# The last expert's rows reach the mixer's first batch through a product with a matrix of ones and zeros

## The chip, the cores and the metric

One core of one Trainium2 chip runs the whole program in one launch. The metric is the device time of the launch in microseconds (us). The engines are TensorE (PE; its weight loads are listed as PEld), VectorE (DVE), ScalarE (ACT), GpSimd (POOL) and SyncE (SP); each runs its own instructions in order and they meet at semaphores. SP issues nearly all plain transfers, POOL the indirect ones (gathers by a list of row numbers).

## The reference

An attention, a mixture of experts and a token and channel mixer follow each other on 4 batches of 576 tokens with 512 features:

```python
x = attention(q, k, v).transpose(0, 2, 1, 3).reshape(B, S, H * D)   # B=4, S=576, H*D=512
for b, s:                                        # experts: one expert e per token
    e = fresh_e if s == 0 or local_gate[b, s] < 0.5 else prev_e
    h = np.maximum(x[b, s] @ w1[e], 0.0)         # 512 -> 1024
    out[b, s] = p[e] * (h @ w2[e])               # 1024 -> 512, p = softmax of the gate
xt = out.transpose(0, 2, 1)                      # mixer
h = np.maximum(xt @ w_tok1, 0.0) @ w_tok2        # over tokens, 576 -> 256 -> 576
u = out + h.transpose(0, 2, 1)
return u + np.maximum(u @ w_ch1, 0.0) @ w_ch2    # over features, 512 -> 1536 -> 512
```

## The kernel before

Three stages use the chip one after another. Each stage records its operations in a `Sched`, which sets the order on every engine by a list of estimated costs and due times and by the buffers that each pool has; the order is fixed when the program is built. All of a helper's operations have the helper's line: L548 a product, L550 a transpose, L552 any other recorded operation, L1168 a gather, L1199 a load of expert weights.

**Experts** (`Moe`, some 200 to 425 us). The eight experts are taken by falling number of tokens; the place of an expert in that order is its rank, and `CAPS` gives the rows that each rank has room for (384, 376, 320, 288, 256, 256, 192 and 128). The routed rows lie in the DRAM table `xd` and are gathered into `xg`; for each rank the hidden size 1024 is cut into 8 chunks. A chunk is one 512 KB load `raw<-in_wx` (4 buffers, SP), its split into a rounded part `wh` (ACT) and a rest `wl` (DVE), a group of products into `m` (`mm1`), a relu with a split into `h` (ACT and DVE), and a group of products that adds into the PSUM banks `y` (`mm2`; four banks, one for each 128 rows of a rank). The last rank, with 128 rows, takes its first products from `raw` itself. After a rank's eighth chunk `mm2` copies each `y` into one of three buffers `yo` (ACT the even ones, DVE the odd ones) and SP stores them to the rank's rows in the DRAM table `yd` (`yd<-yo`, 256 KB each). Beside this, `convert` splits the mixer's weights: load `cr`, four DVE operations on `cf`, one of ACT on `cs`. `zeros()` fills the unused rows of `yd` from a buffer of its own, `zero`.

**Overflow** (L1545). Rows beyond a rank's room are worked off by a loop on the device, whose count `nov` is a runtime value. With these inputs it does not run once, but its start is a place where all engines meet and where SP first waits for every transfer that is still under way. `TAIL` (36) products on constants stand on PE ahead of it (L1537).

**Mixer** (`Mix`, 426 us to the end). For each batch, `token` brings the batch's 576 rows from `yd` in 5 tiles (128, 128, 128, 128 and 64 rows) by gathers with the index `pos`. Each tile is scaled by the gate's probability `pall` twice, on ACT into a rounded part (`f2x<-x_f,pall`) and on DVE in full; DVE subtracts to get the rest; PE transposes the tile (`x_t<-ident,x_f`) and multiplies it into the token mixing (`x_y`). A tile's six products of 128x512 need `f2x` and the rest `f3x`. Filler products on constants (L1752) stand between.

Of the kernel before, what the change touches and what calls it, by code (L numbers as in the profile page):

```python
# [4 lines left out]
F32 = mybir.dt.float32  # L5
F32R = mybir.dt.float32r
# [14 lines left out]
NB5 = 5  # L21
# [6 lines left out]
ROW0 = [128 * sum(TILES[:r]) for r in range(NE)]  # L28
NEARLY, ECAP = 2, 256
ETILES = ECAP // 128  # L30
EROW0 = [128 * sum(TILES) + ECAP * r for r in range(NEARLY)]
OV0 = 128 * sum(TILES) + ECAP * NEARLY
MIN_N = 256
NOV = 16
FF = 1024
# [1087 lines left out]


# [49 lines left out]
class Experts:  # L1174
# [87 lines left out]

    def part(self, C):
# [31 lines left out]
    def mm2(self, r, fb, h):  # L1295
# [27 lines left out]
        if fb == KF - 1:  # L1323
            for k in range(T):
                n = min(128, C - 128 * k)
                t = self.result(r, k)
                if n == m:
                    self.i("act", "copy", out=t[0:n], in_=self.y[k][n:2 * n])
                    self.i("dve", "tensor_tensor", out=t[0:n], in0=t[0:n], in1=self.y[k][0:n], op=ALU.add)
                elif k % 2 == 0:  # L1330
                    self.i("act", "copy", out=t[0:n], in_=self.y[k][0:n])
                else:
                    self.i("dve", "tensor_copy", out=t[0:n], in_=self.y[k][0:n])
                r0 = self.rows[r] + 128 * k
                self.i(self.QUEUE, "dma_start", out=self.yd[r0:r0 + n, :], in_=t[0:n])
# [115 lines left out]
class Moe(Experts):  # L1451
    LO, CUT, QUEUE = "dve", 4, "dma"

    def __init__(self, ctx, tc, at, rt, xd, yd, wx, jobs, lead):
        self.rt, self.xd, self.jobs = rt, xd, jobs
# [13 lines left out]
        for name, ts in tiles.items():  # L1469
            S_.pool(name, [ts[j] for j in sorted(ts)])  # L1470
        for name, n in (("t", 2), ("m", 2), ("y", 4)):
            S_.pool(name, [(pt if name == "t" else pp).tile([128, 512], F32, name=f"{name}{j}") for j in range(n)])
# [18 lines left out]

    def hidden(self, C):
        h, m = self.new("h"), self.part(C)
        return h[:, 0:C], h[:, C:2 * C], h[:, C - m:C + m] if m else None

    def zeros(self):

        zero = self.sp.tile([128, DM], F32, name="zero")
        self.S.i("pool", "memset", out=zero, value=0.0)
        for n in range(0, NOV, 2):  # L1500
            r0 = OV0 + 128 * n
            self.S.i("dma", "dma_start", out=self.yd[r0:r0 + 256, :].rearrange("(i p) w -> p i w", p=128),
                     in_=zero.unsqueeze(1).to_broadcast([128, 2, DM]))
        for r in range(NE):
            n = 128 * TILES[r] - CAPS[r]
            if n:
                self.S.i("dma", "dma_start", out=self.yd[ROW0[r] + CAPS[r]:ROW0[r] + CAPS[r] + n, :], in_=zero[0:n, :])

    def run(self):
# [3 lines left out]
        for n in range(NW):  # L1513
# [12 lines left out]
            if n == 24:  # L1526
                self.S.stage = t0
                self.zeros()
            if n >= 8 and n % CONV == 0 and self.jobs:
                self.S.stage = t0 + 60  # L1530
                convert(self.S, *self.jobs.pop(0), after=(done[n - 6],))
        self.mm2(*prev)
        assert not self.jobs
        self.S.issue(self.S.order(busy=LATE))
        at, cold = self.at, self.S.pools["t"][1][0][:, 264:512]
# [3 lines left out]
    def overflow(self):  # L1539
        tc, nc = self.tc, self.nc  # L1540
        rt, at, p = self.rt, self.at, {n: ts[0][0] for n, ts in self.S.pools.items()}
# [3 lines left out]
        with tc.For_i(0, nov, 1) as j:  # L1545
# [15 lines left out]
            for fb in range(KF):  # L1561
# [5 lines left out]
                h = self.S.pools["cs"][fb % 2][0][:, 0:128]  # L1567
# [4 lines left out]
            nc.sync.dma_start(out=self.yd[bass.ds(OV0 + j * 128, 128), :], in_=yo)  # L1572

# [11 lines left out]
class Mix:  # L1585


    def __init__(self, ctx, tc, at, rt, yd, out, c1, c2, c2t, wt):
# [10 lines left out]
        S_.slots(("f",), sp)  # L1599
        for name, n in (("t", 2), ("m", 2), ("y", 4)):  # L1600
            S_.pool(name, [pp.tile([128, 512], F32, name=f"x_{name}{j}") for j in range(n)])
# [42 lines left out]
    def token(self, b, after=()):  # L1644
# [6 lines left out]
        for j in range(NB5):  # L1651
            n = min(128, S - 128 * j)
            t = S_.next("f")
            gather(S_, t, n, self.yd[:, :], self.rt.pos[0:n, NB5 * b + j:NB5 * b + j + 1], after)
            p = self.at.pall[0:n, b, j:j + 1]
            s = t if b else S_.next("f")
            hi, lo = self.pair() if n == 128 else [S_.next("f", F32R)] * 2
            lo = lo if n == 128 else hi[n:2 * n]
            S_.tie(t, s, hi, lo)
            i("act", "activation", out=hi[0:n], in_=t[0:n], func=AF.Copy, scale=p)  # L1660
            i("dve", "tensor_scalar", out=s[0:n], in0=t[0:n], scalar1=p, scalar2=None, op0=ALU.mult)
# [94 lines left out]
def tile_kernel(tc, qT, kw, vw, vf, wcat, cst, wx, wt, c1, c2, out):  # L1756
    nc = tc.nc
    with ExitStack() as ctx:
# [4 lines left out]
        yd = dp.tile([OV0 + NOV * 128, DM], F32, name="yd")  # L1763
# [29 lines left out]
        for k in range(C2_EARLY):  # L1793
            jobs.append((c2[:, k], DM, *c2t[k]))
        with ExitStack() as a:
            moe = Moe(a, tc, at, rt, xd, yd, wx, jobs, lead)
            moe.run()
            moe.overflow()
        lead_stack.close()
        with ExitStack() as a:  # L1800
            Mix(a, tc, at, rt, yd, out, c1t, c2, c2t, wtt).run()
# [3 lines left out]
TAIL = 36  # L1805
# [8 lines left out]
RING_F, TOK_FB = 26, 3  # L1814
# [29 lines left out]
```

## Time and profile before

| | |
|---|---|
| time, median of 3 runs | 797.12 us (795.53 to 799.46) |
| the profiled execution: time / span | 797.57 us / 795.6 us |
| PE busy | 757.0 us, 95% |
| DVE / ACT / POOL busy | 468.0 (59%) / 333.1 (42%) / 95.4 (12%) us |
| DMA, mean over the span | 136 GB/s |

How to read the rows further down. A line of a timeline has its start and its duration in us, the engine, the line of the program, the operation with output<-inputs and shapes, a count where several stand in a row, and in brackets how long its engine was idle before it and what ended that. SPq is the issue of a transfer by SP. The records of products overlap: the distance of two starts is what a product costs. A line of windows has the stretch, its length, the busy time of PE, PEld, DVE, ACT and POOL (with the number of instructions), the granted clock of TensorE as a share of full speed, the share of the DMA engines and GB/s. In a line of the profile's costliest groups the last fields are busy time and mean ns of one, and the idle time before.

### The profile page before, as it was taken

The page shows a single profiled execution, that of the slowest core. Times are in us where ns is not written, and L with a number is a line of the kernel's source. Part 1 is how long each engine was busy: PE and PEld are TensorE (multiplying, and loading weights), DVE is VectorE, ACT ScalarE, POOL GpSimd, SP SyncE. Part 2 cuts the span into 40 slices and gives each one's busy share as a digit, 9 for nine tenths or more (in the row PEclk, how much of TensorE's full clock was granted, in tenths as well). Part 3 has the DMA queues.
Part 4 walks back from the last instruction along what each step waited for, and adds up shares of the span by engine and source line. Part 5 has one row for each costly group of instructions (what it writes and reads, how often), then busy time and mean ns, then how long its engine had stood idle before and what let it go on. Part 6 is the DMA issues. An engine that isn't in the chain of part 4 may idle for free. (4 is left out here: it accounts for less than half of the span.)

```text
span 795.6 us, 13989 instructions
## 1 busy us (share of the span) xinstructions
PE 757.0 (95%) x5377; PEld 639.8 (80%) x5377; DVE 468.0 (59%) x1093; ACT 333.1 (42%) x722; POOL 95.4 (12%) x100
## 2 busy tenths in 40 slices
PE   7888898799999999999998999999999999999997
PEld 5666686687798988888886888888788878888897
DVE  7779899598667779888953774532242224211121
ACT  1867876544455556565643442312221223011110
POOL 4335311314011010000002000010001000000000
PEclk9989999999999999999999999999999999999999
DMA  9998343649698676777762231020002000000010
GB/s 274 229 215 227 97 137 126 185 140 300 232 346 278 208 269 195 287 244 263 243 213 77 82 97 67 28 80 20 14 1 79 20 14 1 26 28 1 1 54 27
DMA packets 36346, 107.90 MB, mean 136 GB/s; under 512 B 5003, under 2 KB 5643, under 8 KB 35895
## 3 DMA queue, kind: packets, MB, share of 16 engines
q1 hardware_dynamic: 32359, 95.15, 37.4%
q0 software_dynamic: 3200, 10.28, 4.3%
q10 hardware_dynamic: 720, 1.57, 0.6%
q8 instruction: 43, 0.70, 0.4%
q14 instruction: 24, 0.20, 0.1%
HBM read 87.32 MB, written 19.66 MB: 134 GB/s over the span
## 5 line engine op out<-in xcount | busy, mean ns | idle before, releaser
L552 DVE SCALAR_TENSOR_TENSOR x_h<-x_m,x_h 128x512 fp32r<-128x512 f32 (+1 forms) x60 | 38.2, 638 | 194.4 <-ACT x_h L552 194.4
L548 PE MATMUL x_y<-x_h,c2h 128*128 128x512 f32 (+1 forms) x480 | 136.4, 369 | 0.0
L552 ACT ACTIVATE x_h<-x_m 128x512 fp32r<-128x512 f32 (+1 forms) x60 | 33.3, 555 | 206.6 <-PE x_m L548 181.6
L548 PEld LDWEIGHTS x_y<-x_h,c2h 128*128 128x128 f32 x480 | 86.5, 189 | 14.3
L548 PE MATMUL x_y<-x_h,c2l 128*128 128x512 f32 (+1 forms) x240 | 88.3, 368 | 0.0
L548 PE MATMUL y<-wh,h 128*128 128x512 f32 (+2 forms) x206 | 71.8, 400 | 0.2
L552 DVE TENSOR_TENSOR wl<-raw,wh 128x1024 fp32r<-128x1024 f32 (+1 forms) x48 | 54.8, 1143 | 21.6 <-ACT wh L552 20.9
L552 ACT CAST wh<-raw 128x1024 fp32r<-128x1024 f32 (+1 forms) x48 | 47.3, 986 | 31.7 <-PE y L548 25.3
L548 PEld LDWEIGHTS x_y<-x_h,c2l 128*128 128x128 f32 x240 | 45.3, 189 | 7.6
L548 PEld LDWEIGHTS y<-wh,h 128*128 128x128 f32 (+2 forms) x206 | 38.3, 186 | 9.2 <-DVE h L552 1.1
L548 PE MATMUL y<-wl,h 128*128 128x512 f32 (+3 forms) x112 | 41.5, 392 | 0.0
L552 ACT ACTIVATE h<-m 128x256 fp32r<-128x256 f32 (+6 forms) x64 | 25.6, 400 | 22.8 <-PE m L548 22.3
L1168 POOL DMA_INDIRECT xg<-xd,q_xi x19 | 19.4, 1019 | 127.3 <-PE t L550 111.9
L552 DVE SCALAR_TENSOR_TENSOR h<-m,h 128x256 fp32r<-128x256 f32 (+3 forms) x88 | 29.3, 357 | 4.1 <-ACT h L552 4.0
L548 PE MATMUL m<-l_xh,wh 128*128 128x256 f32 (+2 forms) x92 | 28.0, 305 | 1.7 <-DVE h L552 1.6
L548 PE MATMUL pv<-pt,vw 128*64 128x96 f32 x384 | 22.3, 261 | 7.6 <-ACT pt L552 4.6
L552 DVE SCALAR_TENSOR_TENSOR cf<-cr,cf 128x512 int32<-128x512 int32 (+1 forms) x42 | 28.4, 678 | 0.5
L548 PE MATMUL m<-l_xh,wl 128*128 128x256 f32 (+2 forms) x92 | 27.8, 302 | 0.6 <-DVE wl L552 0.6
L548 PEld LDWEIGHTS pv<-pt,vw 128*64 128x64 f32 x384 | 17.6, 142 | 12.6 <-ACT pt L552 5.5
L548 PE MATMUL m<-l_xl,wh 128*128 128x256 f32 (+2 forms) x92 | 27.6, 300 | 0.0
L548 PE MATMUL g<-wcat,xt 128*128 128x137 f32 x160 | 25.1, 299 | 2.0 <-ACT pd L552 1.1
L552 ACT COPY pt<-pc 32x384 f32<-32x384 f32 x48 | 24.4, 508 | 4.8 <-DVE pc L552 4.1
(803 smaller groups left out, 1954.6 us busy)
## 6 DMA issues: line engine op xcount, KB each, us to landing
raw<-in_wx SPq DMA_DIRECT2D x80, 512.0 KB
cr<-in_c SPq DMA_DIRECT2D x16, 512.0 KB
vw<-in_vw SPq DMA_DIRECT2D x12, 512.0 KB
kz<-in_kw SPq DMA_DIRECT2D x24, 200.0 KB
xd<-xn SPq DMA_DIRECT2D x16, 256.0 KB
yd<-zero SPq DMA_DIRECT2D x8, 512.0 KB
yd<-yo SPq DMA_DIRECT2D x15, 256.0 KB
x_cr<-in_c SPq DMA_DIRECT2D x7, 512.0 KB
```

Source lines behind the costliest of these rows:

```text
L548: f(kw.pop("out"), **kw)
L552: f(**kw)
L1168: nc.gpsimd.indirect_dma_start(out=t.real()[0:n, :], out_offset=None, in_=table, in_offset=bass.IndirectOffsetOnAxis(ap=index, axis=0))
```

## The change

- **Routing** makes three more tables for batch 0: `iota`, `place` (a token's place among the last rank's 128 rows, outside 0 to 127 for other tokens) and `pos0` (the token's row in `yd`, or the number of a row of zeros where the token belongs to the last rank).
- **The last rank's rows** move to the end of `yd`, so that a gather from `yd[0:ROW0[-1]]` does not depend on their store.
- **`select`** makes a 128x640 matrix `sel` of ones and zeros: five comparisons of `iota` with `place` on DVE, into two `yo` buffers, five transposes on PE and two copies on ACT.
- **`fetch0`** gathers batch 0's five tiles into `x_e0` to `x_e4` ahead of the loop's end, and ACT scales each by `pall`. They lie in a pool of their own, and serve the mixer as five more `f` buffers.
- **`add0`**, in place of nothing: the last rank's `y` is split into `yh` (ACT) and `yl` (DVE), ten products with `sel` spread its rows over the tokens of five tiles in PSUM, and five DVE operations add `pall` times those to `x_e`. The store of the last rank stays.
- **Mixer**: batch 0 has no gathers; `hi` is an ACT copy of `x_e`, and the DVE scaling is gone. Batches 1 to 3 are as before.
- **Space**: `cs` 2 to 1, `xg` 5 to 3, `RING_F` 26 to 21, no `zero` (`zeros()` uses a `yo`), `TAIL` 36 to 20. In the loop on overflow rows the five tiles are gathered again.

```diff
+        self.place = pp.tile([128, NB5], F32, name="place")
+        v("tensor_single_scalar", out=self.place, in_=row[:, 0:NB5], scalar=-float(ROW0[NE - 1]), op=ALU.add)
...
         if fb == KF - 1:
+            if self.last(r):
+                self.add0()
             for k in range(T):
...
-        zero = self.sp.tile([128, DM], F32, name="zero")
+        zero = self.S.next("yo")
...
+    def select(self):
+        S_ = self.S
+        for j0, j1 in ((0, 4), (4, NB5)):
+            ps = self.new("t").rearrange("p (k n) -> p k n", k=4)
+            a = self.new("yo").rearrange("p (k n) -> p k n", k=4)
+            for j in range(j0, j1):
+                S_.i("dve", "tensor_scalar", out=a[:, j - j0], in0=self.rt.iota, scalar1=self.rt.place[:, j:j + 1], scalar2=None, op0=ALU.is_equal)
+            with S_.group("pe"):
+                for j in range(j0, j1):
+                    S_.i("pe", "transpose", out=ps[:, j - j0], in_=a[:, j - j0], ident=self.ident)
+            S_.i("act", "copy", out=self.sel[:, 128 * j0:128 * j1], in_=ps[:, 0:j1 - j0].rearrange("p k n -> p (k n)"))
+
+    def fetch0(self):
+        S_ = self.S
+        self.f0 = [S_.held("first", t) for t in self.first0]
+        for j, t in enumerate(self.f0):
+            n = min(128, S - 128 * j)
+            gather(S_, t, n, self.yd[0:ROW0[-1], :], self.rt.pos0[0:n, j:j + 1])
+            S_.i("act", "activation", out=t[0:n], in_=t[0:n], func=AF.Copy, scale=self.at.pall[0:n, 0, j:j + 1])
+
+    def add0(self):
+        S_ = self.S
+        y = self.y[0]
+        yh, yl = (self.new("h")[:, 0:DM] for _ in range(2))
+        S_.i("act", "copy", out=yh, in_=y)
+        S_.i("dve", "tensor_tensor", out=yl, in0=y, in1=yh.bitcast(F32), op=ALU.subtract)
+        ps = [self.new("ytmty"[j]) for j in range(NB5)]
+        for part in (yh, yl):
+            for j in range(NB5):
+                n = min(128, S - 128 * j)
+                S_.i("pe", "matmul", out=ps[j][0:n], lhsT=self.sel[:, 128 * j:128 * j + n], rhs=part, start=part is yh, stop=part is yl)
+        for j, t in enumerate(self.f0):
+            n = min(128, S - 128 * j)
+            S_.i("dve", "scalar_tensor_tensor", out=t[0:n], in0=ps[j][0:n], scalar=self.at.pall[0:n, 0, j:j + 1], in1=t[0:n], op0=ALU.mult, op1=ALU.add)
...
+            if n == 40:
+                self.S.stage = t0
+                self.select()
+            if n == NW - KF + 1:
+                self.S.stage = t0
+                self.fetch0()
...
-            t = S_.next("f")
-            gather(S_, t, n, self.yd[:, :], self.rt.pos[0:n, NB5 * b + j:NB5 * b + j + 1], after)
...
+            else:
+                s = self.first[j]
+                i("act", "copy", out=hi[0:n], in_=s[0:n])
...
-TAIL = 36
+TAIL = 20
...
-PLACE = ("cr0 cr1 cf0 cf1 cs0 cs1 yo0 yo1 yo2 h0 h1 h2",
-         "raw0 raw1 raw2 raw3 xg0 xg1 xg2 xg3 xg4 xh0 wh0 wh1 wh2 wl2 wl0 xl0 wl1")
+PLACE = ("cr0 cr1 cf0 cf1 cs0 yo0 yo1 yo2 h0 h1 h2",
+         "raw0 raw1 raw2 raw3 xg0 xg1 xg2 xh0 wh0 wh1 wh2 wl2 wl0 xl0 wl1")
```

What moves in the order is shown at three places. **The end of rank 0, SP's queue** (a number behind a name tells buffers apart). Before, the three stores of rank 0 stand together and use three buffers:

```order
L1199 DMA raw_2763<-in_wx 128x1024
L552 DMA yd<-yo_2756 128x512
L552 DMA yd<-yo_2757 128x512
L552 DMA yd<-yo_2758 128x512
L1199 ISA
L1199 DMA raw_2764<-in_wx 128x1024
L552 DMA cr_2751<-in_wt 128x1024
```

Now, at the same place:

```order
L1214 DMA raw_2782<-in_wx 128x1024
L555 DMA yd<-yo_2775 128x512
L1214 ISA
L1214 DMA raw_2783<-in_wx 128x1024
L555 DMA yd<-yo_2775 128x512
L555 DMA cr_2771<-in_wt 128x1024
L555 DMA yd<-yo_2775 128x512
L555 DMA cr_2770<-in_wt 128x768
```

All three go through the one buffer `yo_2775`, with loads between them; the other two buffers hold the comparisons of `select` from the loop's start until PE has transposed them, which stands in rank 4 for the first and in rank 5 for the second. The same holds at the ends of ranks 1 and 2.

**The end of the loop, ACT.** Before (the last relu, the copy of the last rank's result, the loop on overflow rows):

```order
L552 ACTIVATE h_2760<-m_2782 128x128
L552 ACTIVATE h_2761<-m_2781 128x128
L552 CAST wh_2774<-raw_2764 128x512
L552 ACTIVATE h_2759<-m_2782 128x128
L552 COPY yo_2757<-y_2783 128x512
L1544 TENSOR_LOAD nov
```

Now:

```order
L555 CAST wh_2791<-raw_2783 128x512
L555 ACTIVATE x_e_2753<-x_e_2753,pall 128x512
L555 ACTIVATE x_e_2754<-x_e_2754,pall 128x512
L555 ACTIVATE h_2779<-m_2800 128x128
L555 ACTIVATE x_e_2755<-x_e_2755,pall 128x512
L555 ACTIVATE x_e_2756<-x_e_2756,pall 128x512
L555 CAST h_2780<-y_2803 128x512
L555 ACTIVATE x_e_2757<-x_e_2757,pall 64x512
L555 COPY yo_2776<-y_2803 128x512
L1614 TENSOR_LOAD nov
```

Two scalings now stand ahead of the last relu, two more ahead of the split of the last result, and all five ahead of its copy for the store.

**The mixer's start, PE.** Before, behind 15 of the 17 filler products:

```order
L1752 LDWEIGHTS onesb
L1752 MATMUL x_y_4871<-rb,onesb 128x248
L550 MATMUL x_t_4864<-ident,x_f_4832 128x128 x4
L1752 LDWEIGHTS onesb
L1752 MATMUL x_y_4871<-rb,onesb 128x248
L1752 LDWEIGHTS onesb
L1752 MATMUL x_y_4871<-rb,onesb 128x248
L548 MATMUL x_y_4868<-f2x,wth 128x512
```

Now:

```order
L1615 UNCONDITIONAL_BRANCH
L553 MATMUL x_t_4909<-ident,x_e_2753 128x128 x4
L553 MATMUL x_t_4910<-ident,x_e_2754 128x128 x4
L1838 LDWEIGHTS onesb
L1838 MATMUL x_y_4916<-rb,onesb 128x248
L1838 LDWEIGHTS onesb
L1838 MATMUL x_y_4916<-rb,onesb 128x248
```

The transposes of the first two tiles moved to the front; four fillers follow, and then the token products of all tiles in a row.

## Rows read from the trace of the kernel before

**Rows 1.** The page's first part, busy time of each engine.

```profile
PE 757.0 (95%) x5377; PEld 639.8 (80%) x5377; DVE 468.0 (59%) x1093; ACT 333.1 (42%) x722; POOL 95.4 (12%) x100
```

**Rows 2.** Chain that ended last, around the loop on overflow rows: start, us, what.

```profile
426.53 2.91 DMA x_f<-yd,pos
```

**Rows 3.** Timeline, end of the experts' loop.

```profile
411.87 0.96 SPq L552 DMA_DIRECT2D yd<-yo  x2
...
419.08 0.62 ACT L552 CAST wh<-raw 128x512 fp32r<-128x512 f32 x1 [0.72 <-DMA raw<-in_wx]
419.10 0.97 PEld L548 LDWEIGHTS m<-xg,raw 128*128 128x128 f32 x8 [0.45 <-DMA raw<-in_wx]
...
421.24 0.40 PE L548 MATMUL y<-wh,h 128*128 128x512 f32 x1
...
421.48 3.98 PE L1537 MATMUL t<-rb,onesb 128*128 128x248 bf16 x36
421.68 0.59 ACT L552 COPY yo<-y 128x512 f32<-128x512 f32 x1 [1.11 <-PE y L548]
422.29 0.35 SPq L552 DMA_DIRECT2D yd<-yo  x1
```

**Rows 4.** Timeline, start of the mixer.

```profile
426.53 0.94 POOL L1168 DMA_INDIRECT x_f<-yd,pos  x1 [109.93 <-PEq L1545]
...
427.50 1.97 PE L1752 MATMUL x_y<-rb,onesb 128*128 128x248 bf16 x17 [2.04 <-issue]
427.78 0.94 POOL L1168 DMA_INDIRECT x_f<-yd,pos  x1 [0.30 <-issue]
...
429.93 0.72 ACT L552 ACTIVATE f2x<-x_f,pall 128x512 fp32r<-128x512 f32 x1 [7.67 <-DMA x_f<-yd,pos]
...
430.47 0.66 PE L550 MATMUL x_t<-ident,x_f 128*128 128x128 f32 x4 [0.99 <-DVE x_f L552]
...
431.96 0.72 ACT L552 ACTIVATE f6x<-x_f,pall 128x512 fp32r<-128x512 f32 x1 [1.31 <-DMA x_f<-yd,pos]
...
433.88 0.48 PE L548 MATMUL x_y<-f6x,wth 128*128 128x512 f32 x1
...
434.20 0.39 PE L548 MATMUL x_y<-f7x,wth 128*128 128x512 f32 x1
...
434.43 0.40 PE L548 MATMUL x_y<-f6x,wtl 128*128 128x512 f32 x1
```

**Rows 5.** Windows: before the mixer, in the mixer, and early in the attention.

```profile
45.00:50.00 5.00, 1.62 (x19) 1.35 (x16) 1.68 (x6) 3.41 (x15) 0.00 (x0) 0.74 0.79 170
50.00:55.00 5.00, 5.00 (x45) 4.24 (x43) 3.68 (x12) 3.00 (x15) 4.30 (x4) 0.57 0.98 250
...
425.50:427.50 2.00, 0.00 (x0) 0.00 (x1) 0.00 (x0) 0.00 (x0) 0.94 (x1) 1.00 0.01 4
...
440.00:600.00 160.00, 160.00 (x781) 133.70 (x780) 77.71 (x165) 50.45 (x103) 9.88 (x10) 1.00 0.15 48
```

**Rows 6.** Timeline, end of rank 0, PE.

```profile
247.07 0.85 PE L548 MATMUL y<-l_wh,h 128*128 128x512 f32 x3
...
251.91 0.60 PE L550 MATMUL t<-ident,xg 128*128 128x128 f32 x4
252.27 0.48 PE L548 MATMUL y<-wh,h 128*128 128x512 f32 x1
```

**Rows 7.** Timeline, end of rank 0, SP.

```profile
248.72 1.63 SPq L552 DMA_DIRECT2D yd<-yo  x3
```

**Rows 8.** Timeline, a stall of PE in the loop, and a late weight load.

```profile
386.88 0.19 PEld L548 LDWEIGHTS m<-l_xh,wh 128*128 128x128 f32 x1 [1.82 <-DVE h L552]
...
413.09 0.39 SPq L1199 DMA_DIRECT2D raw<-in_wx  x1
```

**Rows 9.** GB/s in 40 slices of 0.75 us from 395 to 425.

```profile
GB/s 350 98 153 350 197 240 339 246 268 229 202 229 235 93 11 22 0 0 137 289 350 300 262 147 131 229 330 407 421 240 49 27 0 0 0 0 22 183 167 11
```

**Rows 10.** The page's costliest groups: DVE's multiply and add on 128x512.

```profile
L552 DVE SCALAR_TENSOR_TENSOR x_h<-x_m,x_h 128x512 fp32r<-128x512 f32 (+1 forms) x60 | 38.2, 638 | 194.4 <-ACT x_h L552 194.4
```

More of the change, by code (lines that the diff above doesn't have):

```diff
@@ L27 @@
 TILES = [-(-c // 128) for c in CAPS]
-ROW0 = [128 * sum(TILES[:r]) for r in range(NE)]
+ROW0 = [128 * sum(TILES[:r]) for r in range(NE - 1)]
 NEARLY, ECAP = 2, 256
 ETILES = ECAP // 128
-EROW0 = [128 * sum(TILES) + ECAP * r for r in range(NEARLY)]
-OV0 = 128 * sum(TILES) + ECAP * NEARLY
+EROW0 = [128 * sum(TILES[:-1]) + ECAP * r for r in range(NEARLY)]
+OV0 = 128 * sum(TILES[:-1]) + ECAP * NEARLY
 MIN_N = 256
 NOV = 16
+ROW0.append(OV0 + 128 * NOV)
+ZROW = [r0 + c for r0, c in zip(ROW0, CAPS) if c % 128][0]
 FF = 1024
@@ L1261, in result, with last @@
         return self.new("yo")
+    def last(self, r):
+        return False
     def part(self, C):
@@ L1452, with __init__ @@
     LO, CUT, QUEUE = "dve", 4, "dma"
-    def __init__(self, ctx, tc, at, rt, xd, yd, wx, jobs, lead):
-        self.rt, self.xd, self.jobs = rt, xd, jobs
+    def __init__(self, ctx, tc, at, rt, xd, yd, wx, jobs, lead, first):
+        self.rt, self.xd, self.jobs, self.first0 = rt, xd, jobs, first
         S_ = Sched(tc)
@@ L1470, in __init__ @@
             S_.pool(name, [ts[j] for j in sorted(ts)])
+        self.sel = sa.tile([128, NB5 * 128], F32R, name="sel")
+        S_.pool("first", [])
         for name, n in (("t", 2), ("m", 2), ("y", 4)):
@@ L1490, in rows_of, with last @@
         return self.S.next("xh")[:, :, 0:n], self.S.next("xl")[:, :, 0:n]
+    def last(self, r):
+        return r == NE - 1
     def hidden(self, C):
@@ L1572, in overflow @@
             nc.sync.dma_start(out=self.yd[bass.ds(OV0 + j * 128, 128), :], in_=yo)
+            for b, f in enumerate(self.first0):
+                n = min(128, S - 128 * b)
+                nc.gpsimd.indirect_dma_start(
+                    out=f[0:n, :], out_offset=None, in_=self.yd[:, :],
+                    in_offset=bass.IndirectOffsetOnAxis(ap=rt.pos[0:n, b:b + 1], axis=0),
+                )
+                nc.vector.tensor_scalar(out=f[0:n], in0=f[0:n], scalar1=at.pall[0:n, 0, b:b + 1], scalar2=None, op0=ALU.mult)
 def pieces(t0, n):
@@ L1585, with __init__ @@
 class Mix:
-    def __init__(self, ctx, tc, at, rt, yd, out, c1, c2, c2t, wt):
+    def __init__(self, ctx, tc, at, rt, yd, out, c1, c2, c2t, wt, pf, first):
         self.tc, self.nc, self.c2 = tc, tc.nc, c2t
@@ L1599, in __init__ @@
         S_.slots(("f",), sp)
+        self.first = []
+        for j, t in enumerate(first):
+            S_.slot[id(t)] = [t, pf, f"e{j}"]
+            self.first.append(S_.held("f", t))
+            S_.bufs[-1].settled = True
         for name, n in (("t", 2), ("m", 2), ("y", 4)):
@@ L1794, in tile_kernel @@
             jobs.append((c2[:, k], DM, *c2t[k]))
+        pf = pool("pf", 1)
+        first = [pf.tile([128, CN], F32, name=f"x_e{j}", tag=f"e{j}") for j in range(NB5)]
         with ExitStack() as a:
-            moe = Moe(a, tc, at, rt, xd, yd, wx, jobs, lead)
+            moe = Moe(a, tc, at, rt, xd, yd, wx, jobs, lead, first)
             moe.run()
@@ L1800, in tile_kernel @@
         with ExitStack() as a:
-            Mix(a, tc, at, rt, yd, out, c1t, c2, c2t, wtt).run()
+            Mix(a, tc, at, rt, yd, out, c1t, c2, c2t, wtt, pf, first).run()
 WARM, WINDOW = 0.5, 3.4
-TAIL = 36
+TAIL = 20
 NKZ, NVW, NRAW = 5, 4, 3
```

32 lines of the change are left out of this document (22 added, 10 removed).

## The prediction

> **What bounds the kernel now.** I read the busy times first: PE is busy for 757.0 of 795.6 us [rows 1], so time can only come from the few places where PE stands still, or from work of PE that goes away. The windows show where they are not: in the mixer PE is busy for 160.00 of 160.00 us [rows 5], and nothing in the change touches PE's work there. They show one place near the change: from 425.5 to 427.5 PE does nothing [rows 5]. The chain that ended last passes through it by the gather of the mixer's first tile, 2.91 us [rows 2]. The two timelines then give the whole crossing. The last product of the experts starts at 421.24 and lasts 0.40, so I call its end E = 421.64; the fillers of `TAIL` start at 421.48 and end at 425.46 [rows 3]; PE starts again at 427.50 after 2.04 us of "issue", on fillers, while POOL's first gather goes out at 426.53, and ACT gets its data at 429.93, 3.4 us later; the first transposes start at 430.47, the second tile's data is there at 431.96 (4.2 us after its issue at 427.78), and from 433.88 on PE is never short again [rows 4]. Of the 12.24 us from E to 433.88 the needed work is three transposed tiles and six products. A transposed tile costs 252.27 - 251.91 = 0.36 [rows 6], a product 434.43 - 434.20 = 0.23 [rows 4]: 3 x 0.36 + 6 x 0.23 = 2.5. About 9.8 us are waiting or fillers, and this is the most that a perfect crossing could give.
>
> **The change part by part.**
>
> *Crossing, PE after E.* ACT splits `y` (a cast of this size takes 0.62 [rows 3]), so the first product with `sel` starts at E + 0.7. Ten products at 0.23 make 2.3, the DVE subtraction for `yl` beside the first five: E + 3.0. `TAIL` shrinks to 20 of the 36 that took 3.98 [rows 3], or 2.2: E + 5.2. Beside it DVE adds into the five tiles; it may begin when the sixth product is done, E + 2.2, and takes 5 x 0.638 [rows 10] = 3.2: E + 5.4.
>
> *Crossing, the store.* It is still made, and SP still waits for every transfer before the loop on overflow rows. Its copy on ACT now stands behind the split and the last scaling: E + 0.7, then 0.72 [rows 4], 0.59 and the issue [rows 3], E + 2.05. The lone store of before was issued at 422.29 [rows 3], and its traffic ends in the slice that begins at 424.25 [rows 9]; I take a landing of 2.1. That makes E + 4.2, hidden under `TAIL` and DVE, but with one microsecond to spare only.
>
> *Crossing, the restart.* All engines meet at E + 5.4, where before it was E + 3.8. I keep the 2.04 us pause of PE [rows 4]: E + 7.5. Two transposed tiles (0.72) and four fillers at 1.97 / 17 [rows 4] (0.46) follow, since `x_e` is there already and ACT and DVE split its tiles (0.62, and a subtraction like it) faster than the 6 x 0.23 that PE needs for each. Products start at E + 8.6. To stand where before stood at 433.88, six products and a third tile's transposes are missing (1.74): E + 10.4. Before it was E + 12.24: **1.9 us gained at best**.
>
> The Trainium skill, "Runtime: NRT & Kernel Launch", section "Instruction fetch mechanics", says that a taken branch to a page that is not loaded has to wait for a fetch. By it the pause of 2.04 us stays, which is what I assumed; were it a wait for another engine's later arrival that now falls away, the sum would be 2 us lower. The row alone, with "issue" as what ended the pause, does not tell these apart.
>
> *Gathers in time?* They wait for rank 6's stores. Before, those were issued from 411.87 to 412.83 [rows 3]; with 2.1 to land and five gathers 1.25 apart [rows 4] they start at 414.9 to 419.9, and with 3.4 to 4.2 to arrive the fourth is there at 422.1 to 422.9. ACT's order puts four scalings ahead of the split of `y` and two ahead of the last relu. The split would then end at 423.5 to 424.2 in place of 422.3, everything behind it 1.2 to 1.9 later, and the last products up to 0.8 later: gain 0 to 0.7. But the order moves rank 6's last group of `y` ahead by one pair of groups of the last rank: eight weight loads of 0.97 [rows 3] and three products of 0.23, 1.7 us. Then the fourth tile is there at 420.4 to 421.2 and the gathers are just in time. POOL has nothing queued behind them but the load of `nov`. I take **1.4 us gained**, between 0 and 1.9.
>
> *Loop, PE.* Five more transposes, 5 x 0.09 = 0.45, while PE is saturated: **+0.45**. The eleven or so small DVE operations at the start and the two ACT copies to `sel` lie beside PE; I put 0.2 on the path, with 0 and 1 as bounds.
>
> *Loop, `yo`.* Before, three stores leave together [rows 7]. Now the results of ranks 0, 1 and 2 pass one buffer: copy, store, landing L, next copy. At rank 0 the last product ends at T = 247.92 [rows 6]. From there to 251.91 PE did one group of `m` and nine products (2.07) [rows 6], so a group of `m` costs 1.9. Now two such groups and two transposed tiles stand ahead of the next rank's first `y`, T + 4.5, and four products later, T + 5.4, it needs the bank that the second copy empties. That copy ends at T + 0.9 (DVE copy and issue) + L + 0.6. PE does not wait while L is under 3.9 us. The nearest row is the lone store, 2.1; the farthest a 512 KB load among others, issued at 413.09 [rows 8] and used at 419.08 [rows 3], 6.0. A store that is queued behind one 512 KB load adds that load's traffic, 1.3 to 2.6 us at the 200 to 400 GB/s of busy slices [rows 9], to 2.1. I take 3.4 and thus **0**, with up to 2.1 for each of three rank ends.
>
> The Trainium skill, "DMA: Bandwidth & Descriptors", section "Latency and other measured facts", gives 0.2 us of access latency to DRAM on average and 2 us at high load, and names it the main part of a transfer's fixed cost. By that page a landing of 2.1 would become an estimated 3.9 under load, just the limit, and the sum would stay; it speaks against a change that puts landings in a row.
>
> *Loop, the rest.* One `cs` in place of two, three `xg` in place of five: DVE and ACT have slack, and gathers still lead their use. The zeros are stored from a `yo` before the first result needs it, and the mixer still has 26 `f` buffers, 21 and the five tiles. Before lost 1.82 us once to a late weight conversion [rows 8] and 0.45 to a late load [rows 3]; another order of loads may avoid that or make its like. I take 0, between -2.3 and +2.
>
> *Sum*, against the profiled execution's own 797.57 (span 795.6 and 2.0 around it): 797.57 - 1.4 + 0.45 + 0.2 = **796.8**. That execution lies 0.45 above the median of the runs, well inside their spread of 3.9, so I don't shift for it.
>
> **The rivals.**
>
> *Slower: one buffer for the results.* With L at 6.0 each of three rank ends costs 2.1 on PE, 6.3 in all: 803. It decides from L = 3.9 up. For it speaks that the loads in the loop keep the transfer engines busy and that SP now has loads between the stores; against it the 2.1 us of the lone store, and that the next rank's work is brought forward as cover. At L = 5 it is 796.8 + 3.3 = 800.1, still no measurable change.
>
> *It doesn't do what it says.* The store and the gathers take the place of the wait that is removed: the gathers hold up ACT, the split comes late, and the engines meet 1.9 us later than in my sum. Gain 0 or less: 798.2, with the five gathers delaying the last weight loads perhaps 799.
>
> *Faster: the loop's waits go as well.* All of 1.9 at the crossing, and 2.3 of the waits of the loop gone: 797.57 - 1.9 - 2.3 + 0.45 = 793.8; with some of the 2.04 us pause gone too, 792 to 793.
>
> *The clock.* The crossing now has a pause of PE after 20 and not 36 fillers, and no 17 fillers behind it. Early in the attention a window with 1.62 of 5 us busy has a granted clock of 0.74 (a mix of the levels of 1.2 and 2.4 GHz), and the next, fully busy, one of 0.57 [rows 5]: 5 x 0.43 = 2.2 us lost. At the crossing of before, the clock stayed at 1.00 through the idle 2 us [rows 5]. If it falls: 799.0.
>
> **How the numbers follow.** The forecast and its neighbours (gain of 0 to 1.9 at the crossing, small waits) 0.45; gathers late 0.19; clock 0.08; one buffer 0.17, of which 0.15 ends above the bound; faster 0.11. A measurement of this kernel tells about 0.5%, 4 us, from no change, so the bounds are 793.1 and 801.1. Faster 0.11, same 0.74, slower 0.15. The time is that of the forecast. The range leaves out about a tenth at each end: 793.3, the faster case with all waits gone, to 802.0, where L is 5.6 at three rank ends.
>
> **What the profile of the changed kernel would show.** Right: ten products on `sel` right after the last `y`; `x_e` gathers from about 413 on; the last relu not waiting for ACT's scalings; the first `x_t` within 9 us of the last `y`; the clock at 1.00 at the crossing; PE at 20.00 of 20 us from 240 to 340. Wrong: waits of PE on `y` banks or of ACT's `yo` copies on stores at the ends of ranks 0 to 2; the split `h<-y` idle behind a gather; a lower clock behind the crossing; or a mixer that no longer keeps PE busy, in which case the whole sum fails.

## The result and the profile after

The changed kernel took 803.86 us (median, 800.51 to 807.48) against 796.33 us of the kernel before. The ratio on record, which is not the quotient of the two medians (these lie 7.5 us apart), is 1.0081 with an interval of 1.0061 to 1.0101, so **slower by 0.8%, 6.5 us**. The forecast was 796.8 with a range up to 802.0; the time lies outside it. The profiled execution took 806.53 us, with a span of 804.7, 9.1 more than before; it is 2.7 us above its median, so the shares below, which add up to 9.1, describe one execution.

The page of the changed kernel, busy time of each engine, answers to [rows 1]: PE is busy 4.2 us longer, with 16 products fewer.

```profile
PE 761.2 (95%) x5361; PEld 643.0 (80%) x5361; DVE 470.7 (58%) x1106; ACT 336.9 (42%) x730; POOL 96.7 (12%) x100
```

Three landmarks cut the span: the start of the attention's last product (`sl`), E (the end of the last product of the last `y`), and the first 128x288 product of the mixer's token mixing. Between the first two lies the **loop**, between the last two the **crossing** with the mixer's first tiles. The rest of the mixer takes 354.4 to 355.1 us in every kernel of this study; the time ahead of the first landmark, which no experiment aims at, runs from 204.2 to 209.6. The loop grew from 214.06 to 220.98 (+6.9), the crossing from 19.06 to 21.22 (+2.2); that is the whole difference.

The timeline of the changed kernel at the end of the loop (in brackets the idle time before and what ended it), which answers to [rows 3]:

```profile
416.19 0.94 SPq L555 DMA_DIRECT2D yd<-yo  x2
...
421.63 0.94 POOL L1183 DMA_INDIRECT x_e<-yd,pos  x1 [98.42 <-DMA raw<-in_wx]
...
423.63 1.16 PE L551 MATMUL m<-xg,raw 128*128 128x128 f32 x8 [1.41 <-DMA raw<-in_wx]
...
427.49 0.50 PE L551 MATMUL y<-wh,h 128*128 128x512 f32 x1 [0.42 <-ACT x_e L555]
...
428.07 0.40 PE L551 MATMUL y<-wh,h 128*128 128x512 f32 x1
429.85 0.72 ACT L555 ACTIVATE x_e<-x_e,pall 128x512 f32<-128x512 f32 x1 [1.13 <-DMA x_e<-yd,pos]
430.47 0.56 ACT L555 CAST h<-y 128x512 fp32r<-128x512 f32 x1
...
431.09 0.76 PE L551 MATMUL y<-h,sel 128*128 128x512 f32 x1 [2.63 <-ACT h L555]
...
431.65 0.63 PE L551 MATMUL t<-h,sel 128*128 128x512 f32 x1
...
432.08 0.63 PE L551 MATMUL m<-h,sel 128*128 128x512 f32 x1
...
435.09 2.29 PE L1607 MATMUL m<-rb,onesb 128*128 128x248 bf16 x20
...
436.67 0.73 DVE L555 SCALAR_TENSOR_TENSOR x_e<-y,pall,x_e 64x512 f32<-64x512 f32 x1
...
439.42 1.09 PE L553 MATMUL x_t<-ident,x_e 128*128 128x128 f32 x8 [2.04 <-ACT f0x L555]
```

Rank 6's results are stored at 416.19, but POOL's first gather goes out at 421.63, 5.4 us later (the prediction: 3.0). The fourth tile arrives at 429.85, ACT scales it, and only then splits `y` at 430.47, though E is 428.47. PE stands for 2.63 us, and then its products come 0.43 apart (431.65, 432.08), not 0.23.

The windows of the changed kernel (stretch, length, busy time of PE, PEld, DVE, ACT and POOL, granted clock, DMA share, GB/s) at the loop's start, at the crossing and in the mixer:

```profile
212.00:214.00 2.00, 1.57 (x6) 1.58 (x7) 2.00 (x4) 1.39 (x3) 0.00 (x0) 0.68 0.35 57
214.00:216.00 2.00, 2.00 (x7) 1.91 (x6) 1.89 (x5) 0.19 (x1) 0.00 (x0) 0.50 0.64 250
...
430.00:432.00 2.00, 0.91 (x2) 0.80 (x3) 0.69 (x1) 1.86 (x4) 0.00 (x0) 0.79 0.00 0
432.00:434.00 2.00, 2.00 (x6) 1.42 (x5) 0.00 (x0) 0.38 (x1) 0.00 (x0) 0.50 0.37 131
...
450.00:610.00 160.00, 160.00 (x777) 133.72 (x776) 77.15 (x163) 49.38 (x101) 9.85 (x10) 1.00 0.15 48
```

Twice the granted clock falls to 0.50, the 1.2 GHz level, behind a wait of PE. In the mixer PE is as busy as in [rows 5].

The timeline of the changed kernel's loop, where PE waits, with the two rows that lead to the first of these waits and one that leads to the wait at 340.88:

```profile
207.96 0.92 ACTq L555 DMA_DIRECT2D yd<-pc  x2
...
210.07 2.94 ACT L555 CAST wh<-raw 128x1024 fp32r<-128x1024 f32 x3 [1.56 <-DMA yd<-pc]
...
211.17 0.44 PE L551 MATMUL m<-l_xh,wh 128*128 128x384 f32 x1 [1.19 <-ACT wh L555]
...
293.43 0.63 PE L553 MATMUL t<-ident,xg 128*128 128x128 f32 x4 [1.40 <-DMA xg<-xd,q_xi]
...
320.79 0.40 PE L551 MATMUL m<-xh,l_wl 128*128 128x288 f32 x1 [0.64 <-DVE l_wl L555]
...
339.85 0.68 ACT L555 ACTIVATE cs<-cr 128x512 f32<-128x512 f32 x1 [3.66 <-DMA cr<-in_c]
...
340.88 0.50 PE L551 MATMUL y<-wh,h 128*128 128x512 f32 x1 [0.92 <-ACT h L555]
...
345.03 0.36 PE L551 MATMUL m<-l_xh,wh 128*128 128x256 f32 x1 [0.67 <-DVE h L555]
...
350.67 0.51 PE L551 MATMUL y<-wh,h 128*128 128x512 f32 x1 [0.25 <-DVE yo L555]
```

Added up: 1.19 at the start; the clock there, from 212 to 216, 2 x 0.32 + 2 x 0.50 = 1.6; 3.9 in the five waits from 293 to 351; 1.83 in the two at 423.63 and 427.49; 0.45 for the transposes. That is 9.0. Before's loop had a wait of PE that is gone now, in its timeline at the place of [rows 8]:

```profile
386.89 0.39 PE L548 MATMUL m<-l_xh,wh 128*128 128x256 f32 x1 [1.61 <-DVE h L552]
```

That leaves 7.4, against the 6.9 between the landmarks. (The 1.82 of [rows 8] and the 0.45 of [rows 3] are idle times of the weight loads; PE's own row at 419.10 shows no wait.) Of the parts, the 1.41 at 423.63, a late weight load, belongs to no theory below. In the other kernels this wait is 0 to 0.8, and why it is longer here is open.

### The profile page after: what moved, and what is told of

Read it like the earlier page. It is cut to its first block, busy times and chain, and to the rows that moved or that the text cites. A ratio compares the mean times of both kernels' runs of the same rounds, so it can differ in the third digit from the quotient of the medians.

```text
span 804.7 us, 14009 instructions
## 1 busy us (share of the span) xinstructions
PE 761.2 (95%) x5361; PEld 643.0 (80%) x5361; DVE 470.7 (58%) x1106; ACT 336.9 (42%) x730; POOL 96.7 (12%) x100
## 5 line engine op out<-in xcount | busy, mean ns | idle before, releaser
L551 PEld LDWEIGHTS g<-wcat,xt 128*128 128x128 f32 x160 | 21.2, 197 | 6.6 <-DVE lg L555 1.7
```

Of the source, the lines that this page charges most:

```text
L551: f(kw.pop("out"), **kw)
```

## The experiments

Theory 1 for the crossing: the **scalings on ACT**, which wait for late gathers ahead of the last relu and of the split. Theory 2 for the loop: **one buffer `yo`**. Theory 3, formed from the trace after: **where the tiles lie** in SBUF. The tables' new sizes moved `wh0` from bytes 172000 to 176096 of a partition to 177184 to 181280, onto the start of `pc0`, a tile from which the attention's last results are still being stored when the loop starts. Theory 4: the **clock** by itself. Every ratio below is to the kernel before, with its interval.

The loop and the crossing, in us, each from one profiled execution. Some of these lie far from the median of their kernel's runs: shared 5.4 us above, scale 4.2 above, all2 3.0 above, behind 3.7 below. Differences of a few us between two profiles are therefore shown only where the rows name the wait.

| kernel | loop | crossing | ratio of times |
|---|---|---|---|
| before | 214.06 | 19.06 | 1 |
| after | 220.98 | 21.22 | 1.0081 (1.0061 to 1.0101) |
| own | 220.05 | 21.67 | 1.0088 (1.0065 to 1.0111) |
| scale | 216.41 | 21.01 | 1.0016 (0.9983 to 1.0048) |
| both | 216.01 | 18.39 | 1.0036 (1.0011 to 1.0061) |
| loop | 218.87 | 18.74 | 1.0041 (1.0018 to 1.0063) |
| place | 216.54 | 20.40 | 1.0050 (1.0021 to 1.0078) |
| all | 215.12 | 18.34 | 1.0000 (0.9968 to 1.0032) |
| loop2 | 216.79 | 18.79 | 1.0006 (0.9977 to 1.0035) |
| warm | 219.70 | 19.47 | 1.0081 (1.0042 to 1.0120) |
| all2 | 211.53 | 19.97 | 0.9973 (0.9950 to 0.9995) |
| loop3 | 212.35 | 19.26 | 0.9982 (0.9960 to 1.0004) |
| before_pc | 214.83 | 19.06 | 1.0024 (1.0001 to 1.0047) |
| act6 | 211.42 | 19.56 | 1.0005 (0.9974 to 1.0036) |
| shared | 217.54 | 18.44 | 0.9994 (0.9965 to 1.0022) |
| own2 | 214.06 | 20.37 | 1.0019 (0.9993 to 1.0045) |
| behind | 211.06 | 17.75 | 0.9977 (0.9950 to 1.0005) |

**own**: the comparisons and the zeros leave `yo` and lie in the `x_e` tiles.

```diff
+        self.f0 = [S_.held("first", t) for t in first]
...
-        zero = self.S.next("yo")
+        zero = self.f0[2]
...
-            a = self.new("yo").rearrange("p (k n) -> p k n", k=4)
+            a = self.f0[j0 // 4].rearrange("p (k n) -> p k n", k=4)
...
```

> The changed kernel, but the five comparisons and the zeros lie in three of the x_e tiles, so that the results have their three yo buffers from rank 0 on. Theory 1 (the crossing is what costs: the scalings on ACT wait for late gathers, the split of the last result and the products with the selection matrix come late and at half clock): no gain, 803 to 804 us where before runs 796. Theory 2 (the one buffer for the results is what costs, by copies that wait for stores at the ends of ranks 0 to 3): 800 to 802, the waits of ACT on yd<-yo (4.7 us in the profile of the changed kernel) are gone, and PE's waits on h and yo in the loop (0.92, 0.67, 0.25 us) with them.

The waits of PE from 293 to 351 were gone, but the time was that of after. The experiment brought a loss of its own: `x_e2` lies over a buffer of the attention, and the fill with zeros waits for it, with POOL's gathers behind it; ACT's first split then waits for the stores of `pc` until 211.93, 5.7 us after their first issue, where after had 2.1. That the late fill made these stores late is read from the order of the rows. The timeline of own:

```profile
197.58 0.53 POOL L549 MEMSET x_e<- 128x512 f32 x1 [11.37 <-ACT pd2x L555]
198.32 1.06 POOL L1183 DMA_INDIRECT xg<-xd,q_xi  x1 [0.21 <-issue]
...
211.93 1.04 ACT L555 CAST wh<-raw 128x1024 fp32r<-128x1024 f32 x1 [5.09 <-DMA yd<-pc]
...
213.03 0.69 PE L551 MATMUL m<-l_xh,wh 128*128 128x384 f32 x1 [4.72 <-ACT wh L555]
```

The wait at the loop's start became 4.72 in place of 1.19: a second sign that the placement counts.

**scale**: no scalings in the loop; `add0` adds unscaled rows and the mixer scales batch 0 as it does the others.

```diff
-            S_.i("act", "activation", out=t[0:n], in_=t[0:n], func=AF.Copy, scale=self.at.pall[0:n, 0, j:j + 1])
...
-            S_.i("dve", "scalar_tensor_tensor", out=t[0:n], in0=ps[j][0:n], scalar=self.at.pall[0:n, 0, j:j + 1], in1=t[0:n], op0=ALU.mult, op1=ALU.add)
+            S_.i("dve", "tensor_tensor", out=t[0:n], in0=ps[j][0:n], in1=t[0:n], op=ALU.add)
...
```

> The changed kernel without the five scalings on ACT in the experts' loop: the gathered tiles stay unscaled, DVE adds the products' result, and the mixer scales both, as it does for the other batches. Theory 1: the last relu no longer waits (0.85 us), the split follows the last y at once (3.07 us less), the ten products run at 0.23 and not 0.43 us (2 us less), so 799 to 800 us where before runs 796. Theory 2: the crossing was not the loss, 803 us; the copies still wait for stores.

In the trace of scale PE waits 0.68 for the split and the products come 0.23 apart, yet the crossing is 21.01. The last gather lands late, DVE's last addition waits for it, the pause at the restart is 2.81 in place of 2.04, and behind it the clock falls to 0.50. The timeline of scale:

```profile
432.34 0.68 DVE L555 TENSOR_TENSOR x_e<-y,x_e 64x512 f32<-64x512 f32 x1 [1.40 <-DMA x_e<-yd,pos]
...
434.29 1.02 PE L1838 MATMUL x_y<-rb,onesb 128*128 128x248 bf16 x8 [2.81 <-DVEq L1614]
```

**both** is own and scale together.

> Both edits of the runs own and scale together. If theories 1 and 2 each hold for their part: 796 to 798 us where before runs 796. If a third cause (five instead of three gather buffers, one cs, clock at the loop's start) holds most of the loss: 801 us or more.

From own to both, where only the scalings differ, the ratio falls from 1.0088 to 1.0036 and the crossing from 21.67 to 18.39, part of it by the clock, which fell in own's crossing and not in both's: theory 1 holds. From after to scale the ratio falls by 0.65%. The 0.36% that both still loses lies between the two outcomes expected; its wait at the loop's start is 4.38, as in own.

**loop**: the changed loop with the crossing of before; the mixer gathers batch 0 and `TAIL` is 36. The matrix `sel` is made and not used.

```diff
     def last(self, r):
-        return r == NE - 1
+        return False
...
-            if n == NW - KF + 1:
-                self.S.stage = t0
-                self.fetch0()
...
-TAIL = 20
+TAIL = 36
```

> The changed kernel's loop with the crossing of before: select stays, but nothing is gathered ahead, no products are made with the selection matrix, 36 fillers, and the mixer gathers batch 0 itself. Theory 1 alone: 796 to 797 us where before runs 796 (only 0.45 for five transposes). Theory 2 alone: 801 to 803. From the two profiles I expect between them: 799 to 800, since PE's waits in the loop grew by some 2 to 4 us.

Slower than before by 0.41%: half of the loss needs no new crossing.

**place**: another order of the tiles, with `xh0` and `wl2` over `pc` in place of `wh0` and `wh1`.

```diff
-         "raw0 raw1 raw2 raw3 xg0 xg1 xg2 xh0 wh0 wh1 wh2 wl2 wl0 xl0 wl1")
+         "raw0 raw1 raw2 raw3 xg0 xg1 xg2 wh0 xh0 wl2 wh1 wh2 wl0 xl0 wl1")
```

> The changed kernel with another order of buffers in memory alone: wh0 trades places, so that it no longer lies on the buffers pc of the stage before, whose last stores are still under way when the experts' loop starts. Theory 3 (the space that the change took shifts wh0 onto pc, and the loop's first split waits for those stores): PE's wait of 1.19 us at the loop's start and the clock at half behind it go, 2.5 us less than the changed kernel, 801 to 802 us where before runs 796.7. Rival (it is the comparisons on DVE or chance): 804 us, and the wait stays.

The wait of 1.19 is gone, and the clock stays at 1.00 there. 0.3% less than after, with intervals that overlap.

**all** is own, scale and place; **loop2** is loop, own and place.

> The edits of own and scale, and wh0 off pc. If theories 1 to 3 name all of the loss: the loop (from the last product of the attention's rows to the last y) is within 1 us of before's 214.1, the crossing within 1 us of before's 19.1, and the time 795.5 to 797.5 us where before runs 796.7. If three gather buffers, one cs or the five transposes cost more than their 0.45: 798 us or more.

> The kernel of the run loop (the changed loop, before's crossing), with the comparisons and zeros in the x_e tiles and wh0 off pc. Theories 2 and 3 (one buffer for the results, and wh0 on pc, make the whole loss of 3.2 us of the run loop): 796.5 to 797.5 us where before runs 796.7. If the fewer gather buffers or the single cs cost: 798.5 us or more.

All of the loss goes, but the fill with zeros still waits some 11 us in both, and `wl2`, now on `pc`, brought PE a wait of 2.19 at 214.37 in all.

**warm**: 24 filler products between the last `y` and the products with `sel`, which only wait there.

```diff
+        def cover():
+            for _ in range(24):
+                self.nc.tensor.matmul(ps[2].real()[:, 264:512], self.at.onesb, self.at.rb, start=True, stop=True)
...
```

> The changed kernel with 24 filler products on constants between the last y and the products with the selection matrix, where PE waited 2.6 us; the order of everything else is the same. Theory 1b (the pause lets the clock fall, and the ten products run at half speed): the clock stays at 1.00, a product costs 0.23 and not 0.43 us, 1.5 to 2 us less: 802 us where before runs 796.7. Rival (the products hide beside DVE and the store anyway, which end last): 803.5 to 804.

The timeline of warm, products with `sel`:

```profile
425.29 2.72 PE L1567 MATMUL m<-rb,onesb 128*128 128x248 bf16 x24
427.76 0.48 PE L551 MATMUL y<-h,sel 128*128 128x512 f32 x1
428.08 0.39 PE L551 MATMUL t<-h,sel 128*128 128x512 f32 x1
428.31 0.40 PE L551 MATMUL m<-h,sel 128*128 128x512 f32 x1
```

Full speed, 0.23 apart, and a crossing 1.75 us shorter than after's, as theory 4 has it. But this is one profile, and the time, 1.0081 with a wide interval, shows no gain: inconclusive.

**all2**: zeros back in `yo`, the comparisons in `x_e0` and `x_e1`, scale, and an order with `xh0` on `pc`. **loop3** is loop with the same buffers and order.

```diff
-         "raw0 raw1 raw2 raw3 xg0 xg1 xg2 xh0 wh0 wh1 wh2 wl2 wl0 xl0 wl1")
+         "raw0 raw1 raw2 raw3 xg0 xg1 xg2 wh0 wh1 xh0 wh2 wl2 wl0 xl0 wl1")
```

> Like the run all, but the zeros stay in a yo buffer (in the run all their filling waited 11.6 us on GpSimd for buffers of the stage before, with the gathers behind it) and xh0, which is used later, lies on pc in place of wl2 (DVE waited 2.6 us for pc there). If theories 1 to 3 are the whole loss: no PE wait over 0.7 us between 205 and 220 us and the clock at 1.00 there, loop 212 to 214 us, crossing 18.3, time 792 to 794 us where before runs 796. Rival (another wait comes up): no less than the run all, 794 to 796.

> The loop of all2 with before's crossing (mixer gathers batch 0, no products with the selection matrix). It is to tell what the new crossing is worth once the loop costs nothing: if the crossing gains 0.7 us as in the profiles of both and all, this is 0.5 to 1 us slower than all2; if it gains the 1.9 of the prediction's best case, 2 us slower; rival, the crossing gains nothing: the same.

Loops of 211.53 and 212.35: five transposes, three `xg` and one `cs` cost nothing that shows, and the wait of [rows 8] is gone. all2 is the one kernel whose interval lies below 1, only just; among so many kernels that is weak evidence of a gain over before, but it is clearly faster than after.

**before_pc**: the kernel before, with `wh0` and `wh1` exchanged, so that `wh0` lies on `pc`.

```diff
-         "raw0 raw1 raw2 raw3 xg0 xg1 xg2 xg3 xg4 xh0 wh0 wh1 wh2 wl2 wl0 xl0 wl1")
+         "raw0 raw1 raw2 raw3 xg0 xg1 xg2 xg3 xg4 xh0 wh1 wh0 wh2 wl2 wl0 xl0 wl1")
```

> The kernel before with wh0 and wh1 exchanged in memory, so that wh0 lies on pc, and nothing else. Theory 3: PE waits at the loop's start for ACT's first split, 1.2 us or more, and the clock falls to a half behind it: 2 to 3 us slower than before, 798 to 799. Rival (the placement matters only together with the change's other work): the same as before.

The timeline and the windows of before_pc:

```profile
210.85 0.44 PE L548 MATMUL m<-l_xh,wh 128*128 128x384 f32 x1 [1.26 <-ACT wh L552]
...
212.00:214.00 2.00, 1.89 (x8) 1.89 (x9) 2.00 (x3) 1.08 (x2) 0.00 (x0) 0.72 0.49 117
214.00:216.00 2.00, 2.00 (x7) 1.81 (x6) 1.20 (x3) 0.49 (x1) 0.00 (x0) 0.50 0.70 260
```

The same wait, the same fall of the clock, made in a kernel without the change: the mechanism of theory 3 is shown. Its price, 0.24% (0.01 to 0.47%), is only just clear of the noise. The wait of 1.18 to 1.20 also stands in each of after, scale, loop, warm and own2, all with `wh0` on `pc`; with `xh0` there it is absent.

**act6**: all2 with rank 6's stores issued by ACT, past SP's loads.

```diff
-                self.i(self.QUEUE, "dma_start", out=self.yd[r0:r0 + n, :], in_=t[0:n])
+                self.i("act" if r == NE - 2 else self.QUEUE, "dma_start", out=self.yd[r0:r0 + n, :], in_=t[0:n])
```

> all2 with the stores of rank 6 issued by ACT and not by SP. If these stores land late because they stand behind weight loads in SP's own queue: the first x_e gather starts 2.5 to 3.5 us after the stores and not 5 to 6, the last tile is there before DVE needs it, the time is that of all2 or up to 1 us less. If they land late because the transfer engines are busy with loads whichever queue they come from: 5 us as before and the same time.

The timeline of all2, stores and first gather:

```profile
409.60 0.89 SPq L555 DMA_DIRECT2D yd<-yo  x2
...
415.41 0.94 POOL L1183 DMA_INDIRECT x_e<-yd,pos  x1 [67.52 <-DMA raw<-in_wx]
```

The timeline of act6, the same two:

```profile
407.94 0.93 ACTq L555 DMA_DIRECT2D yd<-yo  x2
414.71 0.94 POOL L1183 DMA_INDIRECT x_e<-yd,pos  x1 [68.55 <-DMA raw<-in_wx]
```

From the first issue to the gather 5.8 us by SP, 6.8 by ACT: the queue's place is not the cause. The rows name a weight load as what ended POOL's wait, but in the program this gather waits on the stores of `yd` only; the load is merely the transfer that ended last. In act6 the transfer engines move 382 to 437 GB/s in the slices just before the gather; that it is the loads which delay the stores is argued from this, as no run took the loads away.

**shared**: scale with all2's order of tiles and one `yo` as in after; it differs from all2 in the comparisons' buffers alone.

> all2 with the comparisons in the yo buffers again, so that the results of ranks 0 to 2 share one. Theory 2 (copies wait for stores that land late under load): PE's waits of 0.4 to 1.4 us at 290, 316, 340 and 345 us are back, the loop is 2 to 4 us longer than all2's 211.5, the time 795.5 to 797.5 us where all2 has 793.5 and before 795.7. Rival (waits in the loop are taken up by slack later): the time of all2.

What the profile of shared says of the tile `yo` (who waited for it, us, times):

```profile
  ACT yo L555: 8.0, 6
```

The five waits of PE of after's loop are back, each within 0.21 us of after's (1.61, 0.64, 1.09, 0.66, 0.28), 4.3 us together, and the loop is 6 us longer than all2's, in an execution that lies 5.4 us above the median of shared's runs. In time it is 1.7 us (0.9994 against 0.9973, intervals overlapping).

**own2**: after with the comparisons in `x_e0` and `x_e1`, and no other edit (own's diff without the two lines on `zero`).

> The changed kernel with the comparisons in two x_e tiles and the zeros in a yo buffer, nothing else (the clean form of the run own). Theory 2: the loop's later waits (1.4, 0.64, 0.92, 0.67, 0.25 us) are gone, the wait of 1.19 us at its start and the crossing stay: 2 to 4 us less than the changed kernel, 799.5 to 801.5 us. Rival: 803.5, no gain, as in the run own.

0.62% less than after, and no wait of PE from 215 to 410. That is 4.9 us, more than the 2 to 4 expected; the loop of its profile is 6.9 us shorter, of which 3.9 are the five waits and 1.6 the clock, which here stayed at 1.00 behind the same wait at the start.

**behind**: after with own2's buffers and all2's order of tiles; the scalings stay on ACT, but ordered behind the split of `y`.

```diff
-            S_.i("act", "activation", out=t[0:n], in_=t[0:n], func=AF.Copy, scale=self.at.pall[0:n, 0, j:j + 1])
...
-        S_.i("act", "copy", out=yh, in_=y)
+        k = S_.i("act", "copy", out=yh, in_=y)
...
+        for j, t in enumerate(self.f0):
+            n = min(128, S - 128 * j)
+            S_.i("act", "activation", after=(k,), out=t[0:n], in_=t[0:n], func=AF.Copy, scale=self.at.pall[0:n, 0, j:j + 1])
```

> all2, but with the five scalings back on ACT in the experts' loop, placed behind the split of the last result and its copy for the store, and the mixer as in the changed kernel. Theory 1 (their place ahead of the split is what costs, not the scalings): the split follows the last y at once, the first x_t comes 8.0 to 8.8 us after the last y, time 792 to 794.5 us, as all2 or up to 1 us better. Rival (late gathers hold DVE's additions just as much wherever ACT scales): the engines meet later, 795.5 us or more.

The timeline of behind:

```profile
415.92 0.50 PE L551 MATMUL y<-h,sel 128*128 128x512 f32 x1 [0.68 <-ACT h L555]
...
416.24 3.18 ACT L555 ACTIVATE x_e<-x_e,pall 128x512 f32<-128x512 f32 x5
...
422.74 1.09 PE L553 MATMUL x_t<-ident,x_e 128*128 128x128 f32 x8 [2.04 <-issue]
```

The same five scalings, now behind the split: PE waits 0.68, the clock stays at 1.00, and the crossing is the shortest of all, though the first gather goes out later against E than in after (4.9 us ahead of it, not 6.8). What cost was not the scalings but their place in ACT's queue.

## Why the prediction was wrong

- **"Gathers in time?"** failed. Its landing of 2.1 us came from the one row that was at hand, a lone store at the end of the loop, when the loads had ended. Rank 6's stores leave among the loads, and the gathers followed 5.4 us after the first issue in after, 5.8 in all2; the fourth tile then took 4.5 us from its issue at 425.38, where 3.4 to 4.2 had been reckoned. With 2.4 us more, the margin that the prediction called "just in time" is gone: the last relu came late (0.42 on PE), and the split stood 2.0 us behind E in place of 0. The rival "gathers late" named this mechanism and its place, at 0.19.
- **The clock** was a rival at 0.08, put behind the crossing, at the restart. It fell ahead of that, in the 2.63 us that PE stood for the split, and it stretched the ten products from 2.3 to 4.0 us (431.09 to 435.09). The late split and the clock together make the sum's E + 5.4 for DVE's end into E + 8.9 (437.40).
- **Loop, `yo`, taken as 0,** failed, though not by the reckoning of its rival, whose 803 lies near the measured time by chance. The landing that it turned on, L, was taken as 3.4 with a limit of 3.9. At the ends of ranks 0, 1 and 2 the second copy starts 2.7, 2.3 and 2.8 us after the issue of the first store, so L was below both, and PE did not wait for an emptied bank there (once, 0.25 at 350.67, at the end of rank 3). The third copy starts 4.7, 5.0 and 3.8 us after the issue of the second store, and the prediction left it out. The timeline of the changed kernel at the end of rank 0:

```profile
251.47 0.35 SPq L555 DMA_DIRECT2D yd<-yo  x1
...
254.17 0.61 ACT L555 COPY yo<-y 128x512 f32<-128x512 f32 x1
254.81 0.33 SPq L555 DMA_DIRECT2D yd<-yo  x1
...
259.46 0.59 ACT L555 COPY yo<-y 128x512 f32<-128x512 f32 x1 [1.88 <-DMA yd<-yo]
```

The Trainium skill, "DMA: Bandwidth & Descriptors", section "Latency and other measured facts", with 2 us of latency at high load, had led to an estimate of 3.9. The copies that waited for a store, 2.7 to 5.0 us after its issue, lie on both sides of this, and rank 6's 5.4 to 6.8 are above it; there the measurement decides. What cost PE was what the shared buffer did to the order of the rest. At rank 0 PE did not wait at all; at rank 1 the new order drew two tiles' transposes together, the third tile's gather could go out only once they had freed one of the now three `xg`, at 290.46, and PE had it at 293.43. The relu that PE awaits at 340.88 stood on ACT behind the conversion `cs`, which had waited 3.66 for its load. That these waits come from the shared buffer is shown by own2 and shared; the way from the buffer to each of them is read from the traces alone.

- **"Loop, the rest"** had no term for the start of the loop. The diff shows the new tables, `sel` and the new list of tiles, but where the tiles then lie, and what is still being read there, was not looked at. It cost 1.19 us and, in this execution, 1.6 of clock; before_pc prices it at 0.24%.
- **Right** were the crossing's steps, where the split is in time. In behind, E is 415.24; ten products end at E + 3.2 (sum: E + 3.0), DVE at E + 5.9 (E + 5.4), and the first transposes start at E + 7.5 (E + 7.5). The crossing is 1.3 us shorter than before's; the forecast was 1.4. The pause of PE at the restart stayed, 2.04 us in after, in behind and in [rows 4], and was longer (2.81 in scale, 2.79 in act6) where DVE's last addition came late. What the prediction took from the Trainium skill, "Runtime: NRT & Kernel Launch", section "Instruction fetch mechanics", that a taken branch waits for a fetch, fits this unchanged 2.04; no row shows the fetch itself. The store itself was hidden, the transposes cost no more than their 0.45, and the mixer did not change. The stall of [rows 8] went, as "another order of loads may" had it, though it had cost PE 1.61: the prediction's 1.82 and 0.45 are idle times of the weight loads.

The shares in time don't add up. Taking one cause away from after brings 0.65% (scale), 0.62% (own2) and 0.3% (place), together 1.6%, while all three bring 1.08% (all2). Each edit may also change the order or the waits of the rest, so that each may remove part of what the others remove; no run separates this. A division of the 6.5 us among the causes is therefore left open. So is what the new crossing is worth in time: all2 and behind (0.9973, 0.9977) against loop3 (0.9982) is 0.1% with intervals that overlap, though the crossing of behind is 1.0 to 1.5 us shorter than those of loop, loop2 and loop3 in the traces.

## What to carry to other kernels

An operation that waits for a transfer belongs behind everything on its engine that the critical path needs, and its wait has to be reckoned with the landing time of stores among loads, not of a lone one. A change that takes or frees memory moves every tile behind it: look at what the first writers of the next stage lie on, and whether that is still being stored. Where an edit gives three results one buffer, look at the order that follows from it over the whole loop, not at the one wait that it adds.

## What the runs showed of the hardware

The time from the issue of a store to its landing was not a constant. In shared the profile has it for four stores from `yo`, 2.4 to 5.8 us, two of them stores of zeros. From the first of rank 6's two stores to the gather it was 5.4 to 6.8, whichever queue issued them. In loop2 and in before_pc, where no early gather waits for them, the profile has the landing of the second of these two. What the profile of before_pc says of the tile `yo`, for this one store:

```profile
DMA to landing us min/median/max: 5.6/5.6/5.6
```

The clock falls in one execution and not in another behind the same wait. The windows of all, from 426 on, and then those of all2, each with a pause of PE of 2.04 or 2.05 us that ends at 427.58 and 427.54:

```profile
426.00:428.00 2.00, 0.42 (x4) 0.40 (x5) 0.57 (x2) 1.62 (x3) 0.00 (x0) 1.00 0.02 4
428.00:430.00 2.00, 2.00 (x19) 1.86 (x18) 2.00 (x5) 2.00 (x5) 0.00 (x0) 1.00 0.03 8
```

```profile
426.00:428.00 2.00, 0.47 (x5) 0.44 (x6) 0.36 (x1) 1.41 (x3) 0.00 (x0) 1.00 0.01 4
428.00:430.00 2.00, 2.00 (x13) 1.81 (x11) 2.00 (x5) 2.00 (x4) 0.00 (x0) 0.55 0.03 8
```

In all the clock stays at 1.00; in all2 it is 0.55 and then 0.60 from 430 to 432, and the crossing is 1.6 us longer (19.97 against 18.34). At the loop's start the same wait of 1.18 to 1.26 us left the clock at 1.00 in scale, warm and own2 and halved it in after, loop and before_pc. What decides between the two is open; a single profile can therefore be off by some 2 us per such place, and the times have to speak.
